# One visit per pair for the values products of an attention and two-layer kernel

## Chip, cores and metric

The kernel runs on one core of a Trainium2 chip. The metric is the device time of one execution in microseconds (us), the median of several runs.

## What is computed

Attention over 4 batches of 12 heads (448 positions, 64 per head, soft-capped scores), then two dense blocks on 1792 tokens. The reference, cut to its core:

```
scores = cap * np.tanh(scale * np.matmul(q, k.T) / cap)
attn = np.exp(scores - max);  attn = attn / (np.sum(attn, axis=-1) + 1e-09)
x = np.matmul(attn, v)                    # heads side by side: 1792 x 768
h = (x @ w1) * (x @ w2) @ w3 @ w_out      # 768 -> 1024 -> 1024 -> 768
h = h @ w_in                              # 768 -> 1024
solu = h * softmax(h);  out = (layernorm(solu) * g_ln) @ w_out2
```

All data are 4-byte floats. Only attention up to its normalisation is touched by the change.

## The kernel before

**Pairs and chunks.** The 48 heads are worked on as 24 pairs (`NP`). A pair's 448 keys are cut into four chunks: chunks 0 to 2 hold 128 keys of each of the two heads, and chunk 3 holds the last 64 keys of both heads, the first head's on partitions 0 to 63 and the second's on 64 to 127. `scores` (lines 226 to 239) multiplies keys by queries into PSUM, in three terms of split operands. `exps` (243 to 248) is ScalarE: a tanh in place (L246), then an exponential into SBUF (L247). The tiles `p` of chunks 0 to 2 are 128 x 2 x 448 and have 7 buffers; chunk 3 gives `pl`, 128 x 1 x 448, with 3.

**Values and sums.** For each head the exponentials are multiplied by the values (tile `vd`, 7 blocks of 64 columns) into PSUM tile `o`, head 0 on partitions 0 to 63 and head 1 on 64 to 127, and by ones into PSUM tile `n`, which gives the sums of the softmax. `keep` (250 to 255) has VectorE add chunks 0 and 1 into `s` (L255). `values` (257 to 296) issues all products on one line, L271. Their forms differ. Chunks 0 to 2 take 128 rows by 64 columns, so that the two heads use the two column halves of the array side by side. Chunk 3 takes 64 x 64, out and sums for both heads on the four quarters. The other sums, of `s` and of chunk 2, take 128 rows by 32 columns, four side by side:

```
if c == NCH - 1:
    p = parts[n, c][rows, 0]
    product(out[rows, :S], vs[rows, NV - 1], p, first, last)
    product(outs[n, "sums"][slice(D - j * D, P - j * D), :S], ones[rows], p, True, False)
```

The sums thus stand in two partial sets; `inverse` (298 to 310) moves both to a small tile by two DMAs of POOL's queue (L304), adds them with the guard 1e-9 on VectorE (L307), takes the reciprocal and stores it in DRAM. From there it is later broadcast (L454) and multiplied into the values (L462).

**Order of the work.** The loop at line 683 takes two pairs in three phases. Each phase issues the scores of two chunks, the last keys' scores, the exponentials, and `ahead.step`, which loads, converts (L171 to L173 on VectorE) and splits (L177 ScalarE, L178 VectorE) weights that arrive as 8-byte floats. `fill(ns)` hands TensorE so many ns of independent products: the folding of two weight matrices into one (L369, L387), then the first gated products (L601). Values products come in up to three visits per pair: `last_keys` (chunk 3), `behind` (chunks of a pair whose exponentials are done, with a raised priority) and a plain call for chunk 2; the first `FIRST` pairs take theirs at once. The scheduler orders instructions of an engine by priority and readiness in a simulated timeline at build time; an engine then runs them in that order. `issue_after` ties an instruction behind another on its engine, and within a visit each product is tied to the one before it. The scores stand at a high priority. When the attention is over (about 455 us), the rest of the fill and then the second layer (L765) follow.

Of the kernel before, what the change touches and what calls it, by code (L numbers as in the profile page):

```python
# [9 lines left out]
F32 = mybir.dt.float32  # L10
# [3 lines left out]
ALU = mybir.AluOpType  # L14
# [4 lines left out]
P = 128  # L19
B, H, S, D = 4, 12, 448, 64  # L20
# [5 lines left out]
HALF = 512  # L26
SUMS = 112
# [3 lines left out]

NP, NCH = B * NPAIR, 4
FIRST = 4
NV = 2 * (NCH - 1) + 1
EXPS = 7
FILL = 4600
W3 = 9
WARM = 12
LANDS = 3
# [1 line left out]
SQ = 32  # L41
# [59 lines left out]
def attention_moe_solu(ctx: ExitStack, tc: tile.TileContext, q, k, v, cap, w12, w3t, wo, win, wout2, g_ln, out):  # L101
# [119 lines left out]
        if n < NP:  # L221
            ready[n] = *ready[n], landed.pop(n)

    tiled = [None, None]

    def scores(n, c, place_):

# [22 lines left out]
    def keep(n, c, p):  # L250

        parts[n, c] = p
        if c == 1:
            parts[n, "s"] = t = at.tile([P, 2, S], F32, tag="s", bufs=2, name=f"s{n}")
            dve.tensor_tensor(t, parts[n, 0], p, ALU.add)  # L255

    def values(n, *cs):

        b, m = divmod(n, NPAIR)
        vs = ready[n][4]  # L260
        opening = (n, "out") not in outs
        if opening:
            outs[n, "out"] = ps.tile([P, HALF], F32, tag="o", bufs=2, name=f"o{n}")
        out = outs[n, "out"]
        if 3 in cs:
            outs[n, "sums"] = ps.tile([P, HALF], F32, tag="o", bufs=2, name=f"n{n}")
        seen = [None]

        def product(dst, weights, moving, first, last):
            with tc.issue_after(seen[0].ins) if seen[0] is not None else nullcontext():  # L270
                seen[0] = pe.matmul(dst, weights, moving, start=first, stop=last)  # L271

        for c in cs:
            first, last = opening and c == cs[0], c == NCH - 2
            for j in range(2):
                rows = slice(j * D, (j + 1) * D)
                if c == NCH - 1:
                    p = parts[n, c][rows, 0]
                    product(out[rows, :S], vs[rows, NV - 1], p, first, last)
                    product(outs[n, "sums"][slice(D - j * D, P - j * D), :S], ones[rows], p, True, False)  # L280
                else:
                    product(out[rows, :S], vs[:, j * (NCH - 1) + c], parts[n, c][:, j], first, last)
        if cs[-1] == NCH - 2:
            total = outs.pop((n, "sums"))
            for i in range(4):
                p = parts[n, ("s", NCH - 2)[i % 2]]
                product(total[i * SQ:(i + 1) * SQ, :S], ones[:, :SQ], p[:, 1 - i // 2], False, True)
            t = at.tile([P, S], F32, tag="x", bufs=2, name=f"x{n}")
            if m % 2 == 0:
                xr[b, m // 2] = at.tile([P, 2, S], F32, tag="xr", bufs=3, name=f"xr{b}_{m // 2}")  # L290
            act.copy(t, total[:, :S])  # L291
            act.copy(xr[b, m // 2][:, m % 2], outs.pop((n, "out"))[:, :S])
            inverse(b, m, t)
            for c in (*range(NCH), "s"):
                del parts[n, c]
        tiled[1] = seen[0]

    def inverse(b, m, t):

        w = 4 * S // SUMS  # L300
        if m % 2 == 0:
            inv[0] = at.tile([SUMS, 2, w], F32, tag="inv", bufs=2, name=f"inv{b}_{m}")
        for i in range(2):
            pool.dma_start(out=inv[0][m % 2 * SUMS // 2:, i][:SUMS // 2], in_=t[i * SQ::D])  # L304
        if m % 2 == 1:
            r = inv[0][:, 0]
            dve.scalar_tensor_tensor(r, r, guard[:SUMS], inv[0][:, 1], ALU.add, ALU.add)  # L307
            dve.reciprocal(r, r)
            pool.dma_start(out=r_dr[b, 2 * m - 2:2 * m + 2].rearrange("h s -> (h s)").rearrange("(p w) -> p w", p=SUMS), in_=r)
            stored.add((b, m // 2))  # L310
# [131 lines left out]
    def plan_x(b, parts=range(NPAIR // 2)):  # L442
        for part in parts:
            if (b, part) == (B - 1, NPAIR // 2 - 1):

                plan_again(NF + 2)
            i = len(ahead.items)
            pairs = slice(2 * part, 2 * part + 2)

            def load(i=i, pairs=pairs):  # L450
                rb[i] = early.tile([P, 2, S], F32, tag="rb", name=f"rb{i}")
                for j in range(2):
                    row = r_dr[b].rearrange("(n j) s -> j n s", j=2)[1 - j:2 - j, pairs]
# [200 lines left out]
    if WARM:  # L654
# [6 lines left out]
    pool.memset(ones[:, :SQ], 1.0)  # L661
    pool.memset(ones[:, SQ:], 0.0)
# [11 lines left out]
    def behind(*chunks):  # L674

        with tc.issue_after(tiled[1].ins), tc.high_priority(offset=400):
            values(chunks[0][0], *(c for _, c in chunks))

    def last_keys(n):
        with tc.issue_after(tiled[0].ins), tc.high_priority():  # L680
            values(n, 3)

    for g in range(NP // 2):
        n, first, at_once = 2 * g, g % 2, 2 * g < FIRST
        for phase in range(3):
            run = (((n, 0), (n, 1)), ((n, 2), (n + 1, 0)), ((n + 1, 1), (n + 1, 2)))[phase]
            one, two = (first, 1 - first) if phase != 1 else (1 - first, first)
            with tc.high_priority():
                tiles = [scores(*run[0], one)]
                with tc.issue_after(tiled[0].ins):  # L690
                    tiles.append(scores(*run[1], two))
            if not g and not phase:
                with tc.issue_after(tiled[0].ins):
                    for i in range(WARM // 2):
                        pe.matmul(idle[:, :S], zero[:, 0, :P], zero[:, 0], start=True, stop=True)
            if phase:
                last_keys(n + phase - 1)
            if not at_once and (phase or n > FIRST):
                if not phase:
                    tiled[1] = tiled[0]  # L700
                behind(*(((n - 1, 1), (n - 1, 2)), ((n, 0), (n, 1)), ((n + 1, 0),))[phase])
            for turn, x in enumerate((run[0], (n + phase, 3), run[1])):
                if turn == 1:
                    if phase == 2:
                        continue
                    with tc.high_priority():
                        sc = scores(*x, one)
                else:
                    sc = tiles[turn // 2]
                keep(*x, exps(*x, sc))  # L710
                if g or phase:
                    with tc.issue_after(exp_[0, 1].ins) if not g else nullcontext():
                        ahead.step(2 if g >= NP // 4 else 1)
            if g:
                fill(FILL)
            if at_once or phase == 1:
                values(*run[0])
            if phase != 1 and 0 < n + phase // 2 < NP - 1:
                m = n + 1 + phase // 2
                split_pair(m)  # L720
                take_values(m)
                if m + 1 < NP:
                    with tc.issue_after(loads[max(loads)].ins) if g < 2 else nullcontext():
                        load_pair(m + 1)
            if not g and phase == 1:
                with tc.issue_after(loads[max(loads)].ins):
                    load_pair(2)
            if g:
                fill(FILL / 3)
            if at_once:  # L730
                values(*run[1])
    values(NP - 1, 1, 2)
# [297 lines left out]
def _laid_out(q, k, v, cap, moe_w1, moe_w2, moe_w3, moe_w_out, moe2_w_in, moe2_w_out, moe2_g_ln):  # L1030
# [9 lines left out]
    kt[:, D:, 3 * P + D:] = kt[:, D:, 3 * P:S]  # L1040
    kt[:, D:, 3 * P:S] = 0
    vt = v.reshape(n, 2, S, D)
    last = vt[:, :, 3 * P:].reshape(n, P, 1, D)
# [31 lines left out]
```

## Time and profile before

| | us |
|---|---|
| median of 3 runs | 844.85 (843.99 to 845.64) |
| profiled execution, its own time | 845.83 |
| its span, first to last instruction | 844.1 |
| TensorE busy | 832.6 |
| VectorE busy | 514.0 |
| ScalarE busy | 442.5 |

The profile is of one execution. A float product is recorded as two matmul records, and records of products that run side by side overlap, so the busy time of TensorE is the time that at least one runs. PE is TensorE, PEld its weight loads, DVE VectorE, ACT ScalarE, POOL GpSimd, SP SyncE.

### The profile page before, as it was taken

How to read it: one execution, taken by the hardware profiler on the slowest of the kernel's cores; microseconds unless marked ns; L12 is line 12 of the kernel's file. 1: busy time of each engine (PE TensorE's matmuls, PEld its weight loads, DVE VectorE, ACT ScalarE, POOL GpSimd, SP SyncE). 2: the span in 40 equal slices, each digit the busy share in tenths (PEclk: the TensorE clock that was granted, in tenths of full speed). 3: DMA queues.
4: the chain of work that ended last, by engine and by line, in shares of the span. 5: the costliest groups of instructions: out<-in, count | busy, mean ns of one | idle time of the engine just before them, and what ended most of it. 6: DMA issues, size and time to landing. Idle time of an engine off the chain costs nothing.

```text
span 844.1 us, 11984 instructions
## 1 busy us (share of the span) xinstructions
PE 832.6 (99%) x4379; PEld 635.1 (75%) x4379; DVE 514.0 (61%) x934; ACT 442.5 (52%) x654; POOL 71.0 (8%) x131
## 2 busy tenths in 40 slices
PE   8999999999999999999999999999999999999997
PEld 4565687857545565756577999999888888899997
DVE  6888565774615236536456554443287668888872
ACT  5866675466647466665533231112267666854642
POOL 0110100110111121010100000000002111100000
PEclk9999999999999999999999999999999999999999
DMA  6778654777835435264576679996343334997531
GB/s 209 253 226 264 205 172 119 221 239 272 272 101 184 130 89 202 86 206 160 187 254 210 205 264 379 374 339 200 131 127 113 111 130 111 237 217 159 139 96 75
DMA packets 146570, 161.82 MB, mean 192 GB/s; under 512 B 67440, under 2 KB 120272, under 8 KB 144976
## 3 DMA queue, kind: packets, MB, share of 16 engines
q1 hardware_dynamic: 143056, 155.22, 58.2%
q0 software_dynamic: 3456, 5.84, 3.0%
q8 instruction: 34, 0.56, 0.3%
q14 instruction: 24, 0.20, 0.1%
HBM read 113.25 MB, written 47.53 MB: 190 GB/s over the span
## 4 chain that ended last, share of the span: by engine, by line
PE 86%; DMA 7%; DVE 4%; ACT 2%; issue 1%; SPq 0%; POOL 0%; DVEq 0%; ACTq 0%
PE ab L601 28%; PE u L765 15%; PE o L271 9%; PE v L765 7%; PE f L387 6%; PE sc L238 6%; PE f L369 5%; PE n L271 4%; PE y L765 4%; PE sc L234 2%; DMA ld<-in_wo 1%; DMA ld<-w_dr 1%; DMA wg<-wg_dr 1%; DMA kd<-in_k 1%; DVE cv L173 1%
## 5 line engine op out<-in xcount | busy, mean ns | idle before, releaser
L601 PE MATMUL ab<-xs,wt 128*128 128x448 f32 x1152 | 238.9, 365 | 0.0
L601 PEld LDWEIGHTS ab<-xs,wt 128*128 128x128 f32 x1152 | 214.0, 188 | 28.8 <-issue 12.6
L246 ACT ACTIVATE sc<-sc,qscale 128x896 f32<-128x896 f32 (+1 forms) x96 | 85.0, 887 | 73.7 <-PE sc L238 60.2
L271 PE MATMUL o<-p,vd 128*64 128x448 f32 (+1 forms) x384 | 106.5, 556 | 0.0
L247 ACT ACTIVATE p<-sc,capt 128x896 f32<-128x896 f32 (+1 forms) x96 | 88.1, 920 | 2.4 <-PE o L271 0.7
L369 PEld LDWEIGHTS f<-w,w_o 128*128 128x128 f32 x576 | 71.6, 189 | 23.0 <-issue 8.9
L369 PE MATMUL f<-w,w_o 128*128 128x256 f32 x576 | 79.4, 288 | 2.7 <-DVE w L178 1.1
L765 PE MATMUL u<-ws,a 128*128 128x512 f32 x336 | 80.2, 390 | 0.3 <-DVE a L893 0.3
L765 PEld LDWEIGHTS u<-ws,a 128*128 128x128 f32 x336 | 63.0, 188 | 13.9 <-DVE a L893 0.7
L387 PE MATMUL f<-w_i,w 128*128 128x512 f32 x288 | 71.4, 398 | 0.0
L387 PEld LDWEIGHTS f<-w_i,w 128*128 128x128 f32 x288 | 52.8, 188 | 20.1 <-issue 8.3
L765 PE MATMUL u<-wg,a 128*128 128x384 f32 x336 | 62.0, 334 | 0.0
L765 PEld LDWEIGHTS u<-wg,a 128*128 128x128 f32 x336 | 58.5, 188 | 0.3 <-DVE a L893 0.3
L271 PEld LDWEIGHTS o<-p,vd 128*64 128x64 f32 (+1 forms) x384 | 25.8, 134 | 41.4 <-issue 38.5
L304 POOL DMA_DIRECT2D inv<-x x48 | 31.9, 669 | 293.5 <-ACT x L291 293.5
L609 DVE TENSOR_TENSOR abs<-ab,a 128x448 f32<-128x448 f32 x32 | 19.9, 621 | 56.6 <-PE ab L601 46.0
L605 ACT COPY a<-ab 128x448 f32<-128x448 f32 x32 | 17.1, 533 | 70.9 <-PE ab L601 70.8
L172 DVE SCALAR_TENSOR_TENSOR cv<-ld,cv 128x512 uint32<-128x512 uint32 (+1 forms) x80 | 52.2, 662 | 0.9
L173 DVE SCALAR_TENSOR_TENSOR cv<-ld,cv 128x512 uint32<-128x512 uint32 (+1 forms) x80 | 52.1, 661 | 0.9
L271 PE MATMUL n<-p,ones 64*64 64x448 f32 (+1 forms) x192 | 50.0, 556 | 0.0
L889 ACT CAST a<-s 128x512 fp32r<-128x512 f32 (+1 forms) x42 | 31.3, 754 | 31.2 <-DVE s L911 17.0
L171 DVE TENSOR_SCALAR cv<-ld 128x512 uint32<-128x512 uint32 (+1 forms) x80 | 32.3, 412 | 24.5 <-DMA ld<-in_w 8.8
(133 smaller groups left out, 1124.7 us busy)
## 6 DMA issues: line engine op xcount, KB each, us to landing
ld<-in_w SPq DMA_DIRECT2D x24, 512.0 KB, 4.8
w_dr<-wt SPq DMA_DIRECT2D x6, 1536.0 KB, 7.8
wt<-w_dr SPq DMA_DIRECT2D x6, 1536.0 KB, 9.0
ld<-in_w3t SPq DMA_DIRECT2D x16, 512.0 KB, 4.0
ab_dr<-abs SPq DMA_DIRECT2D x32, 224.0 KB, 4.2
ldx<-ab_dr SPq DMA_DIRECT2D x14, 512.0 KB, 4.5
c_dr<-h SPq DMA_DIRECT2D x14, 512.0 KB, 3.0
ldx<-c_dr SPq DMA_DIRECT2D x56, 128.0 KB, 3.2
```

The lines of the kernel that those rows point to most:

```text
L171: dve.tensor_scalar(x, hi, 5, 2, ALU.logical_shift_left, ALU.logical_shift_right)
L172: dve.scalar_tensor_tensor(x, hi, 0xC0000000, x, ALU.bitwise_and, ALU.bitwise_or)
L173: dve.scalar_tensor_tensor(x, lo, 29, x, ALU.logical_shift_right, ALU.bitwise_or)
L238: tiled[0] = pe.matmul(sc[:, j, :S], keys[rows], qq[rows, :], start=(m == 0), stop=(m == len(terms) - 1))
L246: act.activation(sc[:, :w, :S], sc[:, :w, :S], AF.Tanh, scale=qscale)
L247: exp_[n, c] = act.activation(p, sc[:, :w, :S], AF.Exp, scale=capt)
L271: seen[0] = pe.matmul(dst, weights, moving, start=first, stop=last)
L304: pool.dma_start(out=inv[0][m % 2 * SUMS // 2:, i][:SUMS // 2], in_=t[i * SQ::D])
L369: pe.matmul(f[:, :QW], lw[:, a], rw[:, e], start=(g == 0 and m == 0), stop=(g == NF - 1 and m == 2))
L387: pe.matmul(f, w34[:, a, c, :], rw[:, e], start=(c == 0 and m == 0), stop=(c == NC - 1 and m == 2))
L601: pe.matmul(pp[f, b, i][:, :S], w[:, u], xs[b, c][:, e], start=(c == 0 and m == 0), stop=(c == NC - 1 and m == 2))
L765: pe.matmul(banks[g], a[r][m][:, p, k * P:(k + 1) * P], b[m][:, e, k, :], start=(first and k == 0 and i == 0), stop=(k == NF // 2 - 1 and ...
```

## The change

Each pair's values products come in one visit, `values(n)`, after the scores of phase 2 (first pair) or of the next phase 0 (second pair). All are 128 rows by 64 columns. VectorE adds all four chunks into `s`: chunk 0 + chunk 1 as before, then chunk 3's two 64-partition halves each into its own head's part, then chunk 2. The sums are then one product per head, ones by `s`, at the head of the visit. For chunk 3 the values tile gets an eighth block: each head has its own 128-row block, with zeros on the rows of the other head's keys, so that the exponentials of both heads are multiplied and only one head's count; the host lays the zeros out. The evictions change order (values first, then sums), `inverse` has one DMA, and `fill` is called once per phase with 6100 ns instead of with 4600 and a third of it.

```
-NV = 2 * (NCH - 1) + 1
+NV = 2 * NCH
-FILL = 4600
+FILL = 6100
...
         if c == 1:
             parts[n, "s"] = t = at.tile([P, 2, S], F32, tag="s", bufs=2, name=f"s{n}")
             dve.tensor_tensor(t, parts[n, 0], p, ALU.add)
+            for j in range(2):
+                rows = slice(j * D, (j + 1) * D)
+                dve.tensor_tensor(t[rows, j], t[rows, j], parts[n, NCH - 1][rows, 0], ALU.add)
+        elif c == 2:
+            t = parts[n, "s"]
+            dve.tensor_tensor(t, t, p, ALU.add)
...
-    def values(n, *cs):
+    def values(n):
...
+        out, total = (ps.tile([P, HALF], F32, tag="o", bufs=2, name=f"{x}{n}") for x in ("o", "n"))
...
+        def product(dst, j, weights, moving, first, last):
             with tc.issue_after(seen[0].ins) if seen[0] is not None else nullcontext():
+                seen[0] = pe.matmul(dst[j * D:(j + 1) * D, :S], weights, moving, start=first, stop=last)
+
+        for j in range(2):
+            product(total, j, ones, parts[n, "s"][:, j], True, True)
+        for c in range(NCH - 1):
             for j in range(2):
...
+                product(out, j, vs[:, j * (NCH - 1) + c], parts[n, c][:, j], c == 0, False)
+        for j in range(2):
+            product(out, j, vs[:, 2 * (NCH - 1) + j], parts[n, NCH - 1][:, 0], False, True)
...
+        act.copy(xr[b, m // 2][:, m % 2], out[:, :S])
+        act.copy(t, total[:, :S])
         inverse(b, m, t)
...
-        for i in range(2):
-            pool.dma_start(out=inv[0][m % 2 * SUMS // 2:, i][:SUMS // 2], in_=t[i * SQ::D])
+        r = inv[0]
+        pool.dma_start(out=r[m % 2 * SUMS // 2:][:SUMS // 2], in_=t[::D])
         if m % 2 == 1:
-            r = inv[0][:, 0]
-            dve.scalar_tensor_tensor(r, r, guard[:SUMS], inv[0][:, 1], ALU.add, ALU.add)
+            dve.tensor_scalar(r, r, guard[:SUMS], None, ALU.add)
...
-            if phase:
-                last_keys(n + phase - 1)
-            if not at_once and (phase or n > FIRST):
-                if not phase:
-                    tiled[1] = tiled[0]
-                behind(*(((n - 1, 1), (n - 1, 2)), ((n, 0), (n, 1)), ((n + 1, 0),))[phase])
+            if phase != 1 and n + phase:
+                with tc.issue_after(tiled[0].ins), tc.high_priority(offset=400):
+                    values(n - 1 + phase // 2)
...
             if g:
                 fill(FILL)
-            if at_once or phase == 1:
-                values(*run[0])
...
-            if g:
-                fill(FILL / 3)
-            if at_once:
-                values(*run[1])
-    values(NP - 1, 1, 2)
...
+    values(NP - 1)
```

## Rows read from the trace of the kernel before

**Rows 1.** The page, busy us of each engine (share of the span) and instructions

```profile
PE 832.6 (99%) x4379; PEld 635.1 (75%) x4379; DVE 514.0 (61%) x934; ACT 442.5 (52%) x654; POOL 71.0 (8%) x131
```

**Rows 2.** Windows: stretch, length, busy us by engine, clock, DMA share, GB/s

```profile
0.00:60.00 60.00, 54.92 (x307) 31.04 (x307) 47.19 (x88) 40.55 (x59) 6.61 (x16) 1.00 0.72 228
60.00:105.00 45.00, 45.00 (x284) 27.93 (x284) 33.23 (x62) 28.64 (x44) 4.37 (x7) 1.00 0.75 239
105.00:165.00 60.00, 60.00 (x435) 50.40 (x434) 38.23 (x68) 36.30 (x58) 3.28 (x7) 1.00 0.57 167
165.00:290.00 125.00, 124.09 (x614) 71.32 (x612) 63.12 (x104) 76.39 (x110) 16.59 (x30) 1.00 0.62 199
290.00:455.00 165.00, 165.00 (x836) 104.46 (x835) 86.93 (x159) 90.63 (x133) 19.59 (x34) 1.00 0.54 175
455.00:844.00 389.00, 383.61 (x1913) 349.91 (x1911) 245.30 (x455) 170.03 (x254) 20.51 (x38) 1.00 0.62 190
```

**Rows 3.** Windows of line 271 alone, same columns, TensorE and its weight loads

```profile
0.00:60.00 60.00, 18.12 (x91) 3.58 (x91) 1.00 0.72 228
60.00:105.00 45.00, 17.17 (x78) 3.83 (x78) 1.00 0.75 239
105.00:165.00 60.00, 6.39 (x30) 1.37 (x30) 1.00 0.57 167
165.00:290.00 125.00, 42.47 (x222) 10.24 (x222) 1.00 0.62 199
290.00:455.00 165.00, 53.23 (x252) 12.21 (x252) 1.00 0.54 175
```

**Rows 4.** Timeline of TensorE, 176 to 190 us: start, busy us, what

```profile
176.84 0.59 PE L271 MATMUL o<-p,vd 64*64 64x448 f32 x1
...
177.76 0.47 PE L238 MATMUL sc<-qh,kl 64*128 64x448 f32 x1
...
178.36 2.48 PE L271 MATMUL o<-p,vd 128*64 128x448 f32 x12
180.76 0.56 PE L271 MATMUL n<-s,ones 128*32 128x448 f32 x1
...
181.65 0.73 PE L387 MATMUL f<-w_i,w 128*128 128x512 f32 x2
...
187.92 0.96 PE L271 MATMUL o<-p,vd 64*64 64x448 f32 x2
188.81 1.42 PE L387 MATMUL f<-w_i,w 128*128 128x512 f32 x5
```

**Rows 5.** Timeline of TensorE, 427 to 430 us

```profile
427.68 0.97 PE L271 MATMUL o<-p,vd 128*64 128x448 f32 x4
428.58 0.56 PE L271 MATMUL n<-s,ones 128*32 128x448 f32 x1
```

**Rows 6.** Groups of VectorE by line and form, 0 to 460 us

```profile
L172 DVE SCALAR_TENSOR_TENSOR cv<-ld,cv 128x512 uint32<-128x512 uint32 x63 | 43.0, 689 | 0.7
L173 DVE SCALAR_TENSOR_TENSOR cv<-ld,cv 128x512 uint32<-128x512 uint32 x63 | 43.0, 689 | 0.7
L171 DVE TENSOR_SCALAR cv<-ld 128x512 uint32<-128x512 uint32 x63 | 26.6, 426 | 20.9 <-DMA ld<-in_w 8.8 <-DMA ld<-in_wo 6.3 <-ACT wg L533 2.6
L255 DVE TENSOR_TENSOR s<-p,p 128x896 f32<-128x896 f32 x24 | 26.1, 1089 | 18.2 <-ACT p L247 15.0 <-PE n L271 3.1
...
L216 DVE TENSOR_TENSOR ql<-qd,qh 128x448 fp32r<-128x448 f32 x23 | 14.2, 619 | 0.0
```

**Rows 7.** Groups of all engines by line and form, 0 to 270 us

```profile
L304 POOL DMA_DIRECT2D inv<-x x28 | 18.7, 671 | 160.6 <-ACT x L291 160.6
...
L291 ACT COPY x<-n 128x448 f32<-128x448 f32 x14 | 7.6, 541 | 3.8 <-PE n L271 3.8
```

**Rows 8.** DMA issues: count, KB each, median us to landing

```profile
vd<-in_v SPq DMA_DIRECT2D x24, 224.0 KB, 4.4
```

**Rows 9.** Tile o: matmul ns min/median/max, first and last start us

```profile
L271 PE MATMUL o<-p,vd x384: 536/539/590, 10.8 to 452.3; 128*64 128x448 f32 x144, 64*64 64x448 f32 x48
```

More of the change, by code (lines that the diff above doesn't have):

```diff
@@ L222, in take_values @@
             ready[n] = *ready[n], landed.pop(n)
-    tiled = [None, None]
+    tiled = [None]
     def scores(n, c, place_):
@@ L255, in keep @@
             dve.tensor_tensor(t, parts[n, 0], p, ALU.add)
-    def values(n, *cs):
+            for j in range(2):
[5 more added lines that the diff above has]
+    def values(n):
         b, m = divmod(n, NPAIR)
         vs = ready[n][4]
[L261 to L266, printed above, removed]
+        out, total = (ps.tile([P, HALF], F32, tag="o", bufs=2, name=f"{x}{n}") for x in ("o", "n"))
@@ L267, in values @@
         seen = [None]
-        def product(dst, weights, moving, first, last):
+        def product(dst, j, weights, moving, first, last):
             with tc.issue_after(seen[0].ins) if seen[0] is not None else nullcontext():
-                seen[0] = pe.matmul(dst, weights, moving, start=first, stop=last)
-        for c in cs:
-            first, last = opening and c == cs[0], c == NCH - 2
+                seen[0] = pe.matmul(dst[j * D:(j + 1) * D, :S], weights, moving, start=first, stop=last)
@@ L275, in values @@
+        for j in range(2):
+            product(total, j, ones, parts[n, "s"][:, j], True, True)
+        for c in range(NCH - 1):
             for j in range(2):
[L276 to L295, printed above, removed]
@@ L296, in values @@
-        tiled[1] = seen[0]
+                product(out, j, vs[:, j * (NCH - 1) + c], parts[n, c][:, j], c == 0, False)
+        for j in range(2):
+            product(out, j, vs[:, 2 * (NCH - 1) + j], parts[n, NCH - 1][:, 0], False, True)
+        t = at.tile([P, S], F32, tag="x", bufs=2, name=f"x{n}")
+        if m % 2 == 0:
+            xr[b, m // 2] = at.tile([P, 2, S], F32, tag="xr", bufs=3, name=f"xr{b}_{m // 2}")
+        act.copy(xr[b, m // 2][:, m % 2], out[:, :S])
+        act.copy(t, total[:, :S])
@@ L298, in inverse @@
+        inverse(b, m, t)
+        for c in (*range(NCH), "s"):
+            del parts[n, c]
     def inverse(b, m, t):
@@ L301, in inverse @@
         if m % 2 == 0:
-            inv[0] = at.tile([SUMS, 2, w], F32, tag="inv", bufs=2, name=f"inv{b}_{m}")
-        for i in range(2):
-            pool.dma_start(out=inv[0][m % 2 * SUMS // 2:, i][:SUMS // 2], in_=t[i * SQ::D])
+            inv[0] = at.tile([SUMS, w], F32, tag="inv", bufs=2, name=f"inv{b}_{m}")
+        r = inv[0]
+        pool.dma_start(out=r[m % 2 * SUMS // 2:][:SUMS // 2], in_=t[::D])
         if m % 2 == 1:
-            r = inv[0][:, 0]
-            dve.scalar_tensor_tensor(r, r, guard[:SUMS], inv[0][:, 1], ALU.add, ALU.add)
+            dve.tensor_scalar(r, r, guard[:SUMS], None, ALU.add)
             dve.reciprocal(r, r)
@@ L452, in load @@
                 for j in range(2):
-                    row = r_dr[b].rearrange("(n j) s -> j n s", j=2)[1 - j:2 - j, pairs]
+                    row = r_dr[b].rearrange("(n j) s -> j n s", j=2)[j:j + 1, pairs]
                     pool.dma_start(out=rb[i][j * D:(j + 1) * D], in_=row.to_broadcast([D, 2, S]))
@@ L660, in attention_moe_solu @@
             pe.matmul(idle[:, :S], zero[:, 0, :P], zero[:, 0], start=True, stop=True)
-    pool.memset(ones[:, :SQ], 1.0)
-    pool.memset(ones[:, SQ:], 0.0)
+    pool.memset(ones, 1.0)
     ahead.loads()
@@ L673, in attention_moe_solu, with phases @@
     sync.dma_start(out=gt, in_=g_ln)
[L674 to L684, printed above, removed]
+    def phases(g):
+        n, first = 2 * g, g % 2
         for phase in range(3):
@@ L727, in attention_moe_solu @@
                     load_pair(2)
-            if g:
-                fill(FILL / 3)
-            if at_once:
-                values(*run[1])
-    values(NP - 1, 1, 2)
+    for g in range(NP // 2):
+        phases(g)
+    values(NP - 1)
     close(right)
@@ L1042, in _laid_out @@
     vt = v.reshape(n, 2, S, D)
-    last = vt[:, :, 3 * P:].reshape(n, P, 1, D)
+    last = np.zeros((n, 2, D, 2, D), vt.dtype)
+    for j in range(2):
+        last[:, j, :, j] = vt[:, j, 3 * P:]
+    last = last.reshape(n, P, 2, D)
     vt = vt[:, :, :3 * P].reshape(n, 2, 3, P, D).transpose(0, 3, 1, 2, 4).reshape(n, P, 6, D)
```

## The prediction

> **What bounds the kernel now.** I read the page's head first, then the busy time by stretch, then the same view for the values products alone, then a few visits in the timeline. TensorE is busy 99% of the span [rows 1], and from 60 us to the end hardly anything else is seen on it: 45.00 of 45, 60.00 of 60, 124.09 of 125, 165.00 of 165, at a granted clock of 1.00 (its 2.4 GHz level) in every stretch [rows 2]. So after 60 us an engine that is always issuing sets the time, and what it does not have to do is time saved, as long as its operands come in time. Before 60 us it is idle 5.1 us and VectorE is busy 47.19 of 60; in 60 to 105 VectorE has 33.23 of 45. VectorE is the near rival there, and from 105 on it has room (38.23 of 60, 63.12 of 125, 86.93 of 165) [rows 2]. The stretch after 455 holds no attention.
>
> The values products (line 271) are the part that the change rewrites. They keep TensorE busy for 18.12 + 17.17 + 6.39 + 42.47 + 53.23 = 137.4 us [rows 3], with 28 matmul records per pair (each f32 product leaves two), 24 pairs. By their counts 169 records, or 6.0 pairs, lie before 105 us, 30 (1.1 pairs) in 105 to 165 and 474 (16.9 pairs) after.
>
> **TensorE: one visit per pair.** An unbroken run of twelve 128x64 records starts at 178.36 and the next form starts at 180.76: 2.40 us [rows 4]. Four such records take 427.68 to 428.58: 0.90 us [rows 5]. Eight records more cost 1.50 us, so one costs 0.1875 us beside its twin on the other column half, and 0.15 us per visit is the change of form. After the change a pair has 10 products, 20 records, in one form: 2.40 + 8 x 0.1875 = 3.90 us from start to start, 3.97 in the busy view, which counts the tail of the last matmul (2.48 against 2.40 [rows 4]). 24 x 3.97 = 95.3 us against 137.4, so 42 us less: 35.3 - 6.0 x 3.97 = 11.3 us before 105, 2.1 in 105 to 165, and 95.7 - 16.9 x 3.97 = 28.5 after.
>
> Where this surplus comes from can be seen too. Done at once, the eight last-key records cost no more than one step of the column form: 176.84 to 177.76, 0.92 us [rows 4], against 0.90 for four column records [rows 5]. Zero padding therefore loses nothing: the sums leave this group for their own two products, which replace the eight 128x32 records, 180.76 to 181.65, 0.89 us [rows 4]. By intent the old visit has the same five steps. But it is done in pieces: two 64x64 records alone occupy 187.92 to 188.81 [rows 4], 0.89 us for work worth a quarter of a full group, and every piece pays its own change of form.
>
> I do not expect every new visit to stay whole. The scores are issued at a higher priority and cut old visits in the middle. A cut costs 0.15 us for the change of form, and up to 0.5 us (0.89 - 2 x 0.1875) if it parts two halves of a product. If half of the visits are cut once at about 0.4 us, that is 5 us. The ends are 0 and 10 (all of them cut). Fewer pieces also mean fewer entries for the work before them; no row prices that alone. It lies between nothing and what the visits' own changes of form cost, 24 x 0.15 = 3.6 us; I take nothing.
>
> **VectorE: three adds more per pair.** The 128x896 add exists at 1089 ns, and the change adds another one for chunk 2 [rows 6]. The two half adds, 64 partitions by 448, have no row of their own: nearest is the 128x448 f32 tensor-tensor at 619 ns [rows 6]. If time went with partitions it would be 310, and I take 619, since it has the same length. So 1.09 + 2 x 0.62 = 2.33 us per pair, 56 us in all (41 to 56). After 165 us that is 16.9 x 2.33 = 39 us on 150 of 290: VectorE would stand at 190 of about 262, 72%, off the path. Before 105 it is different: 80.4 busy, plus 6.0 x 2.33 = 14.0, makes 94.4, and a share of 90% gives 105 us. So the 11.3 us that TensorE gains there mostly turn into waits for converted weights, and I count 10 of them as lost. The ends: none lost, if conversions slide into 105 to 165, where VectorE is idle 22 us; and 20 lost, if the adds also lengthen that stretch.
>
> **Small terms.** POOL issues one inverse DMA a pair instead of two, 24 x 671 ns less [rows 7] on a queue that is busy 71.0 us in all [rows 1]: nothing, hidden under the wait for the next pair; one issue, 0.7 us less, if the last pair's chain were bare. The copy of the sums now stands behind the copy of the values, so that chain starts one copy, 541 ns [rows 7], later: hidden by the fill products, at worst 24 x 0.54 = 13 us if each normalisation were late, which no wait of TensorE now shows. The values load grows from 224 to 256 KB [rows 8], 0.79 MB in all: nothing, since a pair's values are wanted only at its visit; uncovered it is about 4 us at the 190 GB/s or so of these stretches [rows 3]. SP's queue gets no more issues. The guard's add only loses an operand. The fill per phase goes from 4600 + 1533 to 6100, in 33 phases 1.1 us of products that move behind the attention; their sum stays.
>
> **What is late next.** Each visit starts with the sums, so it now waits for the last add of its pair, behind the exponential of chunk 2 on ScalarE and whatever conversion stands before it in VectorE's queue. Behind it on TensorE wait the products of that visit, and behind these the evictions on ScalarE. The fill products cover this if they are ordered ahead of the visit.
>
> **Sum.** 845.8 (the profiled execution's own time, 1.0 above the median of 844.85) - 42 + 5 + 10 = 818.8; as a median, 818. The ends: -42 with 3.6 us of entries and the 1.0 of the median gives 799, and I put the low end at 801; 10 for cuts and 20 for VectorE gives 845.8 - 42 + 30 - 1 = 833. Not all bounds of the small terms (0.7, 4 and 13 us) can fall due together; 5 us of them make 838.
>
> **Rivals.**
> - *All of it arrives* (chance 0.15): VectorE's early stretch gives no loss and few cuts happen: 801 to 807. For it: VectorE's 22 idle us in 105 to 165 [rows 2]. Against it: VectorE's 47.19 us of the first 60 and TensorE's 5.1 idle us there.
> - *The visits are still cut, or their steps do not pair* (0.13): the change does not do what it says. 20 records then cost about what 28 did less a third, 10 to 15 us gained at most: 830 to 840.
> - *The visit waits for VectorE* (slower 0.10, no change 0.02). Place: the first sums product of each visit. Price: the add queued behind one whole conversion, 0.43 + 0.69 + 0.69 + a subtraction of about the same [rows 6], 2.5 us; if TensorE's fill is ordered behind the visit, 24 x 2.5 = 60 us, so 845.8 - 42 + 60 = 864. It decides from 42 / 24 = 1.75 us per visit on. For it: VectorE already stood idle 15.0 us before the present adds, waiting for ScalarE [rows 6]. Against it: TensorE shows almost no idle time with the present adds [rows 2], and this wait would need to come on every visit.
>
> - *Other engines set the pace up to 290 us* (0.05). VectorE up to 105, where its 14.0 us of adds are then paid in full; ScalarE, busy 76.39 of 125 us [rows 2], in 165 to 290; and only after 290 does TensorE's saving count, 53.23 - 9.0 x 3.97 = 17.5 us [rows 3]: 845.8 + 14.0 - 17.5 - 1 = 841. For it: TensorE's idle time before 60. Against it: TensorE is not idle in 105 to 290 but for 0.9 us [rows 2], and an engine that waits for another would be.
>
> The Trainium skill speaks for this last rival (Perfetto Trace Analysis, "Identifying the Most-Contended Engine"): it holds the busy share of matmuls to be no good measure of how near TensorE is to its limit, and asks for the busy share of its weight loads instead. By that rule TensorE stands behind VectorE up to 105 us (31.04 against 47.19, then 27.93 against 33.23) and behind ScalarE in 165 to 290 (71.32 against 76.39 [rows 2]), and the sum would be 841. The trace agrees before 60 us, where TensorE does idle, and not after.
>
> **Numbers.** Forecast 0.55 (its own range 808 to 833), the others as above. Faster: 0.55 + 0.15 + 0.13 + 0.05 = 0.88; slower 0.10; no change 0.02, within 0.2% (1.7 us), about what a measurement of this kernel can tell. The range of 801 to 838 leaves out the wait for VectorE, the pace of other engines, and a little of the cut visits.
>
> **What would show it.** Right: 480 records of values products, about 95 us busy instead of 137, in about 24 to 36 pieces; VectorE's busy time up by 56 us; the last values products near 425 instead of 452.3 [rows 9], with some 392 us from there to the end, as now; TensorE idle up by some 10 us before 105 and hardly after. Wrong: idle time of TensorE at line 271's first record released by VectorE's add, a half add far from 0.62 us, or a visit of 20 records longer than 4.2 us.

## The result and the profile after

The changed kernel takes 823.95 us (median of 4 runs, 822.26 to 826.25) against 845.25 for the kernel before: a ratio of 0.9747, 95% interval 0.9716 to 0.9779. It is 21.3 us faster. The forecast was 818, with a range of 801 to 838.

The page of the profiled execution (824.29 us by its own time) gives the balance. Its second fenced line is the busy time of each engine:

```profile
span 822.5 us, 11645 instructions
...
PE 800.3 (97%) x4187; PEld 639.9 (78%) x4187; DVE 564.5 (69%) x1006; ACT 442.6 (54%) x654; POOL 55.8 (7%) x106
```

The span falls from 844.1 to 822.5, 21.6 us. TensorE is busy 832.6 - 800.3 = 32.3 us less [rows 1], and idle 22.2 us instead of 11.5, so 10.7 of the 32.3 are given back as idle time. VectorE has 564.5 - 514.0 = 50.5 us more. Where this lies is seen in the windows of the changed kernel; the columns are those of [rows 2], and 432 us is where its attention ends:

```profile
0.00:60.00 60.00, 50.79 (x269) 32.64 (x271) 51.21 (x92) 42.23 (x59) 4.34 (x12) 0.89 0.68 218
60.00:105.00 45.00, 40.99 (x281) 32.51 (x278) 39.33 (x74) 23.57 (x40) 1.64 (x3) 0.96 0.76 241
105.00:165.00 60.00, 58.39 (x403) 43.14 (x402) 43.99 (x75) 39.80 (x59) 3.61 (x6) 1.00 0.54 165
165.00:290.00 125.00, 123.42 (x599) 81.21 (x598) 83.14 (x133) 81.91 (x121) 13.82 (x27) 0.99 0.68 218
290.00:432.00 142.00, 141.51 (x724) 99.04 (x723) 101.24 (x182) 83.91 (x124) 13.30 (x24) 1.00 0.58 191
432.00:822.00 390.00, 385.20 (x1921) 351.40 (x1919) 245.57 (x455) 171.14 (x256) 19.08 (x35) 1.00 0.62 190
```

TensorE is idle 60 - 50.79 = 9.2 us in the first 60 (5.1 before [rows 2]) and 4.0 in 60 to 105 (none before), then 1.6, 1.6 and 0.5. VectorE is busy 51.21 of the first 60 us, 39.33 of the next 45. TensorE's granted clock, the column behind POOL's, is 0.89 and 0.96 in these two stretches, where it was 1.00. The values products alone, now on line 272, answer to [rows 3]:

```profile
0.00:60.00 60.00, 13.37 (x62) 4.58 (x64) 0.89 0.68 218
60.00:105.00 45.00, 7.75 (x40) 2.49 (x36) 0.96 0.76 241
105.00:165.00 60.00, 14.05 (x60) 4.33 (x60) 1.00 0.54 165
165.00:290.00 125.00, 29.27 (x144) 9.42 (x144) 0.99 0.68 218
290.00:432.00 142.00, 37.42 (x176) 12.13 (x176) 1.00 0.58 191
```

Their sum is 101.9 us against 137.4, with 480 records instead of 672. The timeline of TensorE around two visits, to be held against [rows 4]:

```profile
175.61 0.97 PE L272 MATMUL n<-s,ones 128*64 128x448 f32 x4
176.41 3.18 PE L272 MATMUL o<-p,vd 128*64 128x448 f32 x16
179.51 2.11 PE L378 MATMUL f<-w_i,w 128*128 128x512 f32 x8
181.56 0.97 PE L272 MATMUL n<-s,ones 128*64 128x448 f32 x4
182.46 0.96 PE L378 MATMUL f<-w_i,w 128*128 128x512 f32 x3
```

and around a third:

```profile
142.37 3.22 PE L272 MATMUL o<-p,vd 128*64 128x448 f32 x14
...
146.32 0.96 PE L272 MATMUL o<-p,vd 128*64 128x448 f32 x2
```

The first visit is whole: 20 records in one form, 175.61 to 179.51, 3.90 us. The second is cut behind its sums: 181.56 to 182.46, 0.90 us for four records, which is the price of four records in any visit [rows 5]. This cut falls between two steps and costs one more change of form. The third visit is cut between the two products of a step: the last product goes alone, and its two records are busy 0.96 us, as long as the four at 175.61 (0.97). Of the 34 unbroken pieces in which the visits are done, eight hold an odd number of products, and in each of these half of the array stands empty beside one product, which costs about 0.375 us (2 x 0.1875). On VectorE the three adds of a pair, the half adds on line 258 and the new full one on line 261:

```profile
L258 DVE TENSOR_TENSOR s<-s,p 64x448 f32<-64x448 f32 x48 | 29.5, 614 | 4.0 <-ACT p L247 3.5
...
L261 DVE TENSOR_TENSOR s<-s,p 128x896 f32<-128x896 f32 x24 | 25.9, 1080 | 0.8 <-ACT p L247 0.8
```

A half add of 64 partitions takes 614 ns, as long as a subtraction of 128 partitions of the same length (619 [rows 6]).

### The profile page after: what moved, and what is told of

The parts are those of the page before. It is cut to its first block, busy times and chain, and to the rows that moved or that the text cites. A ratio compares the mean times of both kernels' runs of the same rounds, so it can differ in the third digit from the quotient of the medians.

```text
span 822.5 us, 11645 instructions
## 1 busy us (share of the span) xinstructions
PE 800.3 (97%) x4187; PEld 639.9 (78%) x4187; DVE 564.5 (69%) x1006; ACT 442.6 (54%) x654; POOL 55.8 (7%) x106
## 4 chain that ended last, share of the span: by engine, by line
PE 74%; DVE 11%; DMA 10%; issue 3%; ACT 1%; SPq 0%; POOL 0%; DVEq 0%; POOLq 0%
PE ab L592 26%; PE u L741 15%; PE v L741 8%; PE f L378 6%; PE o L272 6%; PE y L741 4%; PE sc L238 4%; PE f L360 3%; DVE cv L173 2%; DMA qd<-in_q 2%; DVE cv L172 2%; PE n L272 2%; DMA inv<-x 1%; DMA ld<-in_win 1%; DMA wg<-wg_dr 1%
## 5 line engine op out<-in xcount | busy, mean ns | idle before, releaser
L272 PE MATMUL o<-p,vd 128*64 128x448 f32 x384 | 80.7, 541 | 0.0
L378 PE MATMUL f<-w_i,w 128*128 128x512 f32 x288 | 73.1, 402 | 1.6 <-ACT w L177 1.3
L378 PEld LDWEIGHTS f<-w_i,w 128*128 128x128 f32 x288 | 53.1, 190 | 21.6 <-issue 8.4
L272 PEld LDWEIGHTS o<-p,vd 128*64 128x64 f32 x384 | 27.9, 138 | 45.6 <-issue 44.1
L600 DVE TENSOR_TENSOR abs<-ab,a 128x448 f32<-128x448 f32 x32 | 19.9, 622 | 58.2 <-PE ab L592 48.0
L255 DVE TENSOR_TENSOR s<-p,p 128x896 f32<-128x896 f32 x24 | 26.1, 1087 | 22.1 <-ACT p L247 22.1
L741 PE MATMUL v<-ws,a 128*128 128x512 f32 x168 | 40.4, 389 | 0.0
```

The source lines that it names most:

```text
L272: seen[0] = pe.matmul(dst[j * D:(j + 1) * D, :S], weights, moving, start=first, stop=last)
L378: pe.matmul(f, w34[:, a, c, :], rw[:, e], start=(c == 0 and m == 0), stop=(c == NC - 1 and m == 2))
L741: pe.matmul(banks[g], a[r][m][:, p, k * P:(k + 1) * P], b[m][:, e, k, :], start=(first and k == 0 and i == 0), stop=(k == NF // 2 - 1 and ...
```

## Experiments

Two questions were open. Which part pays: the single visit, the single form, or only both? And is the time that TensorE gives back lost to VectorE's adds, to the order, or to the clock? Each ratio is against the kernel before, run on the same chip.

**The adds taken out of the changed kernel, and put into the kernel before.** In the first, the lines of the half adds and of chunk 2's add go:

```
-            for j in range(2):
-                rows = slice(j * D, (j + 1) * D)
-                dve.tensor_tensor(t[rows, j], t[rows, j], parts[n, NCH - 1][rows, 0], ALU.add)
-        elif c == 2:
-            t = parts[n, "s"]
-            dve.tensor_tensor(t, t, p, ALU.add)
```

> The changed kernel without VectorE's three further adds per pair (the sums then hold chunks 0 and 1 only; all else stays). Theory A (the adds load VectorE while weights are converted, so the fold starts late and TensorE idles, with its clock falling): the fold's first step ends 8 us or more sooner (some 158 us into the run instead of 166), TensorE's idle time of 22 us falls to some 12, time 808 to 815. Rival B (the adds are hidden; the early loss comes from one late visit per pair, which leaves TensorE without work): time 822 to 825, idle time as in the changed kernel.

In the second, the kernel before gets three adds of the same shapes into a tile that nothing reads:

```
+            parts[n, "extra"] = e = at.tile([P, 2, S], F32, tag="e", name=f"e{n}")
+            for j in range(2):
+                rows = slice(j * D, (j + 1) * D)
+                dve.tensor_tensor(e[rows, j], t[rows, j], parts[n, NCH - 1][rows, 0], ALU.add)
+        elif c == 2:
+            e = parts.pop((n, "extra"))
+            dve.tensor_tensor(e, parts[n, "s"], p, ALU.add)
```

> The kernel before with three adds of the same shapes per pair on VectorE, whose result nothing reads. Theory A: 56 us more VectorE time, the early stretch up to 105 us becomes longer, 8 to 14 us: 853 to 859. Rival B: hidden, 844 to 847.

Without the adds: 815.96 us, ratio 0.9655 (0.9638 to 0.9671), 8.0 us below the changed kernel. With the adds alone: 854.91, ratio 1.0113 (1.0095 to 1.0130), 9.4 us above the kernel before. So the adds cost 8 to 9 us from either side, and they are not hidden. Theory A's range is met in the second and missed by 1 us in the first. But TensorE's early idle time is not the adds', as that theory has it. The windows of the kernel without adds:

```profile
0.00:60.00 60.00, 50.35 (x261) 31.69 (x261) 47.36 (x88) 39.75 (x57) 4.21 (x12) 0.91 0.71 230
60.00:105.00 45.00, 41.74 (x292) 30.66 (x293) 37.66 (x70) 29.93 (x48) 2.64 (x5) 1.00 0.76 240
...
165.00:290.00 125.00, 125.00 (x607) 80.35 (x606) 72.25 (x120) 82.82 (x122) 14.49 (x30) 1.00 0.67 219
290.00:440.00 150.00, 150.00 (x766) 110.09 (x765) 90.45 (x173) 85.15 (x124) 11.71 (x20) 1.00 0.61 202
```

TensorE is still idle 9.7 and 3.3 us up to 105, as with the adds (9.2 and 4.0). Gone is the idle time from 165 to 440 (125.00 of 125 and 150.00 of 150), which was 2.1 us. Idle time is the smaller part of what the adds cost, as the page of this kernel shows:

```profile
PE 795.9 (98%) x4187; PEld 636.8 (78%) x4187; DVE 513.0 (63%) x934; ACT 442.9 (54%) x654; POOL 55.8 (7%) x106
```

Its span is 815.8 us, 6.7 below the changed kernel's 822.5. TensorE's idle time is 19.9 us against 22.2, which is 2.3 of the 6.7; the other 4.4 are busy time of the same 4187 records (795.9 against 800.3). The mean granted clock is 0.994 instead of 0.988. With levels of 1.2 and 2.4 GHz that means an estimated 10 us at the lower level (815.8 x 0.006 x 2) instead of 20 (822.5 x 0.012 x 2), and 10 us less at half speed are worth some 5 us, about what the records gained.

**The adds taken out for the first 6 pairs alone**, which are the pairs of the stretch in question (`range(2 if n >= 6 else 0)` and `c == 2 and n >= 6` in the lines above):

> The changed kernel without the three adds for the first 6 pairs alone (their sums hold chunks 0 and 1 only). If the 8 us that the adds cost lie in the stretch where VectorE is busy nine tenths: 815 to 819. If most of them lie later, in the second half of the fold: 821 to 825.

826.56 us, ratio 0.9768 (0.9731 to 0.9804): nothing gained, and above both ranges. The first half of the fold does end sooner. The view of the tile of its weights says at the end of the line when its products start for the first and the last time; before, changed, without any adds, without the first pairs' adds:

```profile
L369 PE MATMUL f<-w,w_o x576: 274/281/393, 19.5 to 158.9; 128*128 128x256 f32 x192
```

```profile
L360 PE MATMUL f<-w,w_o x576: 276/281/582, 25.0 to 167.3; 128*128 128x256 f32 x192
```

```profile
L354 PE MATMUL f<-w,w_o x576: 274/280/582, 18.6 to 162.3; 128*128 128x256 f32 x192
```

```profile
L360 PE MATMUL f<-w,w_o x576: 274/280/580, 18.7 to 160.6; 128*128 128x256 f32 x192
```

So 6.7 us are won by then (167.3 to 160.6), and 5.0 without any adds (to 162.3). In the kernel without the first pairs' adds they are lost again afterwards, as its windows and its waits of TensorE from 165 us on show:

```profile
0.00:105.00 105.00, 92.52 (x567) 63.14 (x569) 86.22 (x158) 71.19 (x107) 6.86 (x16) 0.95 0.74 242
...
165.00:290.00 125.00, 121.56 (x575) 78.00 (x574) 79.96 (x127) 78.70 (x115) 13.16 (x26) 0.97 0.66 215
290.00:430.00 140.00, 136.17 (x685) 94.78 (x684) 95.26 (x171) 80.33 (x117) 12.57 (x22) 0.99 0.55 183
```

```profile
PE f L378 <- ACT w L177: 3.0, 1, 3.0
PE ab L592 <- ACT a L596: 2.3, 1, 2.3
```

TensorE is idle 3.4 us in 165 to 290 and 3.8 in 290 to 430, and waits for ScalarE's split of a weight block for 3.0 us at once. Why it waits there can be followed in the changed kernel, which has the same wait of 1.3 us. First a part of the chain of waits in 190 to 200 us (start, us, what), then TensorE's timeline beside it:

```profile
190.62 0.68 DVE cv L173
...
191.34 5.51 DMA ld<-w_dr
...
196.87 0.84 ACT w L177
...
197.73 0.97 DVE w L178
```

```profile
193.66 2.77 PE L378 MATMUL f<-w_i,w 128*128 128x512 f32 x11
197.75 0.73 PE L378 MATMUL f<-w_i,w 128*128 128x512 f32 x2 [1.32 <-ACT w L177]
```

VectorE's conversion (line 173) frees a landing buffer at 191.3; only then can the next block of folded weights be loaded (5.51 us); then ScalarE and VectorE split it, and TensorE, which has had nothing left since 196.4, goes on at 197.75. Right behind this wait the granted clock falls: 0.57 in 199 to 203 us, mostly its lower level, after 1.00 in 192 to 199. (The weights that are converted are 8-byte floats, 512 KB for a block of 128 x 512, so "All data are 4-byte floats" above does not hold for them.) What stands ahead of that conversion in VectorE's queue, the adds among it, would delay a transfer and not only VectorE's own results. That is an explanation read from one chain, and no run tests it.

Where the adds cost their time can be read from the fold's second half; changed, without any adds, without the first pairs' adds:

```profile
L378 PE MATMUL f<-w_i,w x288: 387/389/628, 168.0 to 283.6; 128*128 128x512 f32 x144
```

```profile
L372 PE MATMUL f<-w_i,w x288: 387/389/504, 162.5 to 274.5; 128*128 128x512 f32 x144
```

```profile
L378 PE MATMUL f<-w_i,w x288: 387/389/792, 160.7 to 274.4; 128*128 128x512 f32 x144
```

Without any adds the fold is 5.0 us ahead at its middle and 9.1 at its end, and nothing is won behind it: the last values product starts at 421.6 instead of 430.6, 9.0 sooner. In the changed kernel the adds thus cost their time before 284 us, more than half of it before 167. Without the first pairs' adds the fold ends as early, 274.4, but the last values product starts at 433.1. In the kernel before, the three adds put the fold's end back by only 3.2 us (289.3 to 292.5) and the last values product by 8.5 (452.3 to 460.8). So the adds cost about the same in both kernels, in different places. Which of them cost it is not shown: no kernel leaves out the later pairs' adds alone, and the scheduler orders all instructions anew for every kernel, whose own effect on the time is not measured.

**One visit with the old forms**: the changed kernel's order, the products of the kernel before. The eight last-key records, the 128x64 records and the eight 128x32 records of a pair stand in one visit; no adds, two inverse DMAs:

```
+            for j in range(2):
+                rows, p = half[j], parts[n, NCH - 1][half[j], 0]
+                product(out[rows, :S], vs[rows, 2 * (NCH - 1) + j], p, True, False)
+                product(total[half[1 - j], :S], onesh[rows], p, True, False)
...
+            for i in range(4):
+                p = parts[n, ("s", NCH - 2)[i % 2]]
+                product(total[i * SQ:(i + 1) * SQ, :S], onesh[:, :SQ], p[:, 1 - i // 2], False, True)
```

> One visit per pair as in the changed kernel, but with the products of the kernel before: last keys on quarters of the array, sums by 128x32 products, no further adds on VectorE, two inverse DMAs. Theory A (the saving is that pieces are gone, not the form): a whole visit of 28 records takes 4.2 us against 3.9, values products busy some 105 to 110 us, no early loss from adds: 811 to 820. Rival C (the saving is the single form, since changes of form cost more than 0.15 us each): values products stay near 130 us busy and the time near 840.

844.31 us, ratio 0.9987 (0.9971 to 1.0004): no difference, although the adds are absent. Both theories missed. The values products, over the whole attention, are busy 120.1 us, between what A and C expected:

```profile
0.00:470.00 470.00, 120.12 (x672) 30.44 (x672) 0.97 0.61 196
```

and a visit in its timeline shows the larger part of the reason:

```profile
310.85 0.96 PE L274 MATMUL o<-p,vd 64*64 64x448 f32 x2
311.74 0.67 PE L610 MATMUL ab<-xs,wt 128*128 128x448 f32 x2
312.34 0.59 PE L274 MATMUL n<-p,ones 64*64 64x448 f32 x1
...
316.54 1.48 PE L610 MATMUL ab<-xs,wt 128*128 128x448 f32 x6
```

The two records at 310.85 are the first product of the visit; they go alone, 0.89 us, then other work, then the rest, 312.34 to 316.54, 4.20 us. 11 of its 40 pieces are such lone pairs of records (14 of 83 in the kernel before), 11 x 0.89 = 9.8 us that theory A did not count. In the old forms the first product fills one quarter of the array and its three neighbours are separate products, so a cut there leaves three quarters empty.

The 17 us that the values products do save do not reach the time. Its page:

```profile
PE 819.8 (97%) x4379; PEld 638.2 (76%) x4379; DVE 513.3 (61%) x934; ACT 444.0 (53%) x654; POOL 70.6 (8%) x131
```

With a span of 843.4 us, TensorE is busy 12.8 us less than before [rows 1] and idle 23.6 us instead of 11.5: what it saves comes back as idle time, 13.0 us of it up to 105 (5.1 before) and 4.5 in 330 to 380, both at a clock of 0.90. At equal adds, that is none, the new form is worth 28 us in the same order (844.31 to 815.96).

**The same with the sums product first.** The two lines of the last keys change places:

> One visit per pair with the old forms, but the last keys' sums product stands ahead of the values product in each half. Theory F (the two lone 64x64 records of 0.89 us arise because the values' PSUM buffer is freed one eviction earlier than the sums', so the first product goes alone and the scheduler puts other work between): most of the 15 lone pieces go, values products busy some 105 us instead of 119, time 829 to 836. Rival (they arise from the operands or the priority): as many pieces, 842 to 847.

840.15 us, ratio 0.9941 (0.9922 to 0.9959), values products busy 117 us. As many lone pieces (11) as in the last kernel, now of the sums (the 15 and 119 us of the expectation are 11 and 120.1 by the trace): whichever product comes first goes alone. So the order of the evictions, theory F's cause, is not it, and what holds the second product back is left open. The 4 us are a little more than what the values products lost in busy time.

**The new form in the old order**: the kernel before with its three visits, but all products 128x64, the zero-padded values, one sums product per head at the end of the last visit, and the adds:

```
                 if c == NCH - 1:
-                    p = parts[n, c][rows, 0]
-                    product(out[rows, :S], vs[rows, NV - 1], p, first, last)
-                    product(outs[n, "sums"][slice(D - j * D, P - j * D), :S], ones[rows], p, True, False)
+                    product(out[rows, :S], vs[:, 2 * (NCH - 1) + j], parts[n, c][:, 0], first, last)
...
+            for j in range(2):
+                product(total[j * D:(j + 1) * D, :S], ones, parts[n, "s"][:, j], True, True)
```

> The kernel before in its order of visits (up to three per pair), but with the changed kernel's products: zero-padded last keys, all on 128x64, one sums product per head, and the three adds. Theory G (the single form is what pays: no half-filled groups can be left alone, and one visit by itself gave nothing): values products busy some 105 to 110 us instead of 137, and 820 to 830. Rival A (the visits pay): 838 to 850, since the adds cost 9 us and the pieces stay.

834.61 us, ratio 0.9873 (0.9830 to 0.9915), values products busy:

```profile
0.00:460.00 460.00, 107.03 (x480) 30.02 (x480) 0.99 0.62 202
```

107.0 us, as G expected, though the time is above G's range and below the rival's. Half of what TensorE saves comes back as idle time: on the page of this kernel it is busy 807.1 us, 25.5 less than before, and idle 25.1 of 832.2, which is 13.6 more. With it the four corners are complete: old order and old forms 845, one visit alone 844, the form alone 835, both 824. The form brings most of TensorE's saving (137 to 107 us busy, of 137 to 102). The two corners with the new form carry the adds, the other two do not; against the old order with the adds alone (854.91) the form is worth 20 us. The visit is worth 11 us with the new form, of which up to 3 may be the fill's (below), and 1 with the old one.

**The first pairs in the old way.** Two kernels ask whether the early loss comes from the order of the first pairs. In one the first 6 pairs take the old products in their one visit, without adds; in the other the first 4 take the old products in the old order as well.

> The changed kernel, but the first 6 pairs take the products of the kernel before in their one visit and get no further adds on VectorE. Theory A: the early stretch as in the kernel with old forms throughout, the rest as changed, so faster than both: 806 to 816. Rival B: 822 to 826, since the adds were hidden.

> The changed kernel, but the first 4 pairs take their values products as in the kernel before: chunk by chunk behind the exponentials, old forms, no further adds. Theory D (the early loss that the adds do not explain comes from the single late visit: with nothing to do TensorE idles 9 us of the first 60 and its clock is halved for 20 us in all): idle time of the first 60 us back to some 5, granted clock 1.00 there, 814 to 820. Rival E (ScalarE's and VectorE's chains set the first 100 us, whatever TensorE does there): 823 to 832, as with old forms in the first 6 pairs.

831.01 us (ratio 0.9831, 0.9807 to 0.9856) and 826.71 (0.9781, 0.9759 to 0.9802): neither is better than the changed kernel. The first is above both of its ranges, the second where rival E had it. In the second, TensorE's idle time up to 105 us falls to 105 - 98.24 = 6.8 us, near what theory D said, and nothing is gained by it. This one execution was granted a clock of 0.95 in nearly all stretches, at which records last longer, so a part of the 6.8 may be the clock's; its other three executions had 0.99 to 1.00 and took 824 to 827 us.

```profile
0.00:105.00 105.00, 98.24 (x580) 0.95 0.72 235
```

The fold's first half ends at 162.3, as without adds and 5.0 us sooner than in the changed kernel, but 165 to 210 has 3.2 us idle again. Less idle time in the first 105 us does not shorten the whole here; whether the cut visits take that time or something later does is not separated.

**TensorE kept at work.** Six products on zeros after the scores of each of the first phases, to hold up the clock:

```
+            elif g < 2:
+                with tc.issue_after(tiled[0].ins):
+                    more = ps.tile([P, HALF], F32, tag="f", bufs=2, name=f"idle{g}_{phase}")
+                    for i in range(WARM // 2):
+                        pe.matmul(more[:, :S], zero[:, 0, :P], zero[:, 0], start=True, stop=True)
```

> The changed kernel with 6 further products on zeros after the scores of each of the first phases (five times, about 1.2 us each at full clock), written to PSUM and read by nothing; the zeros keep a buffer of their own. If the halved clock itself costs what it seems to (up to half of 20 us): the clock stays at 1.00 to 60 us and the time is 816 to 821. If only the waits count: 823 to 828, the products being in the way.

830.89 us, ratio 0.9852 (0.9818 to 0.9886), though the clock of the first 60 us rises from 0.89 to 0.97:

```profile
0.00:60.00 60.00, 50.22 (x272) 33.15 (x274) 48.57 (x88) 39.48 (x55) 4.35 (x12) 0.97 0.63 209
```

The time is above both ranges. TensorE is still idle 9.8 us there, with 24 of the 30 further products in this stretch, and in 60 to 105 it is idle 7.9 us (4.0 in the changed kernel) at a clock of 0.92. The fold's first half ends at 173.6 instead of 167.3, 6.3 us later, about what 30 products take at full clock (5 x 1.2 us). So the products stood in the way, and holding up the clock for 60 us did not pay for them. What the lower clock costs there by itself isn't separated by this.

**The half adds on GpSimd** (`pool.tensor_tensor` for `dve.tensor_tensor` on that line):

> The changed kernel with the two half adds per pair on GpSimd instead of VectorE. If the adds cost by VectorE's time: 29.5 of its 55 us go, about half of the 8 us: 818 to 821. Rival: GpSimd is so slow at it, or gets in VectorE's way so much, that the sums come later: 825 to 835.

837.83 us, ratio 0.9914 (0.9899 to 0.9929), 14 us worse than the changed kernel and above both ranges. One add takes 1442 ns there, and the sums come later, so that TensorE waits at the head of the visit:

```profile
L258 POOL TENSOR_TENSOR s<-s,p 64x448 f32<-64x448 f32 x48 | 69.2, 1442 | 121.0 <-DVE s L255 99.1 <-PE n L272 11.7 <-DVE w_o L178 4.3
```

```profile
PE n L272 <- DVE s L261: 9.7, 4, 3.4
```

This is the prediction's slower rival in small: 9.7 us of such waits where the changed kernel has 2.1.

**The two small terms.** The copies in the old order, and the fill of the kernel before (4600 ns and a third of it at the end of the phase):

> The changed kernel with the copy of the sums ahead of the copy of the values again. My small term says hidden: 823 to 826. If the normalisation were late, up to 13 us less.

> The changed kernel with the fill of the kernel before: 4600 ns and a third of it at the end of the phase. My small term says no change: 823 to 826. If where the fill is issued decides how the visits are cut, more pieces and 828 or more.

823.49 us (ratio 0.9733, 0.9698 to 0.9768) and 826.78 (0.9779, 0.9743 to 0.9816). The order of the copies makes no difference. The kernel with the old fill has 33 pieces, no more than the changed one; its interval overlaps the changed kernel's, so up to 3 us may be the fill's and may be nothing. None of these kernels that computes the whole is measurably faster than the changed kernel.

## Why the prediction was right

**The bound.** TensorE after 60 us was the right place to look: the last values products start at 430.6 instead of 452.3, and from there to the end it is 392 us in both, so the gain lies before it.

**One visit, one form.** The term was -42 + 5 = -37 us; 137.4 - 101.9 = 35.5 was measured. A whole visit took the 3.90 us that two rows had given. There are 34 pieces, within the 24 to 36 named. The ten cuts fall into 7 visits and cost an estimated 4.5 us, 10 x 0.15 for the changes of form and 8 x 0.375 for products parted from their twin; the text had priced them at 5. Two early visits took 4.4 and 4.6 us, at 20.5 and 33.8 us with the clock at its lower level for a part of each: longer than the 4.2 that the text named as a sign of being wrong, but not for the reason meant. The Trainium skill (TensorEngine Tiling (Array Packing), "Key Properties") says that a change of the tiling mode drains TensorE. The trace agrees with 0.15 us per visit. The lone products of the old forms show that this was the smaller part of the matter.

The explanation of the surplus was half right. The lone pieces of 0.89 us were named. But the text made the pieces a matter of the visits, and there it failed: one visit with the old forms left 11 where there had been 14, and gained nothing. The new form makes a cut cheaper and not impossible: a lone product takes about 0.9 us in either form, but it is half of a step in the new form and a quarter in the old one, and the changed kernel has two of them. Why none of its visits begins with one is not shown.

**VectorE.** Three adds of 1.09 and 2 x 0.62 us were forecast, 1.08 and 2 x 0.61 measured; the upper of the two ends was right, as time did not go with partitions. They take 25.9 + 29.5 = 55.4 us. The page's total rose by only 50.5, since it counts time in which two records of VectorE overlap once; the sum of all their lengths rose by 54.7.

**The early loss.** 10 us were taken off for TensorE's idle time, and it grew by 10.7. Up to 105 us it grew by 8.1 (13.2 against 5.1). The amount was right, and by luck, since the reason given, VectorE's adds, is not the one: without any adds TensorE idles 12.9 us in that stretch (105 - 50.35 - 41.74), though VectorE is then busy 85.0 of the 105 us and not 90.5, and without the first pairs' adds 105 - 92.52 = 12.5. The waits of the changed kernel up to 165 us name ScalarE's exponentials (line 247) most, and not converted weights:

```profile
PE sc L238 <- ACT p L247: 5.0, 4, 1.7
PE f L360 <- ACT w L177: 1.6, 1, 1.6
PE n L272 <- DVE s L261: 1.6, 1, 1.6
```

So in the first 105 us the attention's own chain sets the pace more than the conversions do, as far as the waits show it, and what TensorE saves there becomes idle time with or without the adds. The adds cost 8 us beside that, and only partly as idle time: 2.3 us of it, the rest in records that last longer at the lower clock. Half of it or more lies before 167 us, as the text's worse end ("if the adds also lengthen that stretch") had it, and the rest before 284, where VectorE's share of 72% had put the adds "off the path". Two effects, the early idle time and the cost of the adds, were counted as one of 10 us; what the sum leaves out by that is in the next paragraph.

**What was left out.** The sum was 818.8 on the profiled execution's scale, 824.3 was measured. Of the 5.5 us between them, 1.5 are the values products, 0.7 the idle time, and 3.2 are TensorE's other products, which the prediction left alone: all together TensorE is busy 32.3 us less, the values products 35.5. The windows show a granted clock of 0.89 and 0.96 up to 105 us, and of 0.99 in 165 to 290, against 1.00; records in such stretches take longer, as the two early visits show. The prediction has no term for the clock. The profiled execution stands 0.3 us above the median of the runs (824.29 against 823.95).

**The rivals.** "All of it arrives" is out by the early idle time. "The visits are still cut" did happen, ten times, and cost an estimated 4.5 us; its price, 10 to 15 us gained, does not follow from its own words, since a third less of 137.4 us is 46. "The visit waits for VectorE" cost 2.1 us in two waits, far from 42; the GpSimd kernel shows what it looks like when it counts. "Other engines set the pace up to 290" (841) holds for the place up to 105 us, though not for its reason, the adds, and not from 165 on, where TensorE is idle 2.1 us, its values products fell from 95.7 to 66.7 us and the attention ended 21.7 us sooner.

## What to carry to other kernels

Pack small products in a form with few parts to a step: where a scheduler may put other work between two instructions, a product of a group of four quarters that is left alone leaves three quarters of the array empty, one of a pair of halves leaves half, and a cut between two pairs costs only the change of form. Work added to an engine that is busy 61% of the time is not free: here three adds per pair cost 8 to 9 us. Ask which buffers that engine's queue frees, as a transfer may hang on them. When a saving vanishes, look at the clock beside the idle time, since both may carry the loss. And a saving on the busiest engine counts only in the stretches where that engine does not already wait; here a quarter of it (8.1 of 32.3 us) was lost in the first 105 us, and 7.8 us without the added work.

## What the hardware showed beside it

An add on VectorE of 64 partitions by 448 takes 614 ns, a subtraction of 128 partitions 619: half the partitions save nothing. The same half add on GpSimd takes 1442 ns, in a trace whose times on GpSimd are rough. In the first 60 us the changed kernel, whose TensorE idled 9.2 us there, was granted a clock of 0.89, the kernel without adds 0.91 at 9.7 us, the kernel before 1.00 at 5.1, and the one with products on zeros 0.97 at 9.8; so the length of the idle time alone doesn't set it. The two levels behind these means are 1.2 and 2.4 GHz.
